# A third crossbar buffer, later chunk loads, and crossbar and store traffic counted in a static order: linear attention followed by a two-layer network

## The chip, the cores and the metric

The kernel runs on one core of a Trainium2 chip. The metric is the device time of one execution in microseconds (us), as the median of several runs. Five engines work side by side: TensorE (PE), VectorE (DVE), ScalarE (ACT), GpSimd (POOL) and SyncE (SP), which here only issues transfers. Each engine executes its own instruction list strictly in order, and so an instruction that waits holds up all that stands behind it on that engine.

## The reference, cut to what matters

```python
# q, k, v: (4, 8, 768, 64); blocks of 64 positions along the sequence
for b in range(nb):
    intra = einsum('bhic,bhjc->bhij', qb, kb) * Dmask      # lam ** (i - j), causal
    intra = einsum('bhij,bhjd->bhid', intra, vb)
    inter = einsum('bhid,bhde->bhie', qb * lam_pow, kv_state)
    out[:, :, sl] = intra + inter
    kv_state = lam_block * kv_state + einsum('bhsd,bhse->bhde', kb * rev_pow, vb)
x = out.transpose(0, 2, 1, 3).reshape(3072, 512)
h = x @ w_in                                                # 512 -> 2048
g = where(h >= 1, h, where(h <= -1, 0, (h + 1)**2 / 4))     # smoothed relu
result = g @ w_out                                          # 2048 -> 512, float32
```

## The kernel before, in words

The work is cut into 24 chunks of 128 positions (six for each of the four batches, all eight heads together) and six stages of 512 tokens (four chunks each). Attention produces a chunk's 128 columns of the transposed activations xT. The network then runs over the stages: L1 (f_l1, L368) multiplies by w_in into a PSUM tile ph, ACT applies the relu with bias (f_r, L376), DVE makes the smoothed relu of two such tiles in three instructions (f_g1 L382, f_g2 L386, f_g3 L401) into gT, and L2 (f_l2, L407) multiplies by w_out into py, which ACT copies out (f_y, L412) and SP stores (f_st, L416). An L1 item and an L2 item are each 2048 columns on PE; there are 96 of each.

The first four chunks are transposed on PE. Chunks 4 to 23 take another way, and these are what the change touches. SP loads k, q and v of the chunk (f_load, L450; names x1f, x0f, x2f; 256 KB each, six buffers of each). ACT (three quarters) and DVE (one quarter) cast k into a block-diagonal tile (f_ki, L262 and L264), DVE writes the scaled q beside it (f_qn, L267): together the tile kq, of which there are three. SP then issues one transpose through the DMA crossbar (f_xt, L273) from kq into a tile xq; the pool xtp has NXT = 2 of these. PE computes scores from xq (f_s, L324, eight matmuls of 64 columns), DVE masks them (f_m, L331, tile sc), and PE computes the chunk's output po from sc, v and the state (f_o, L349 and L351), reading xq once more. ACT copies po into xT (f_x, L358). Beside it, POOL scales v (cast_v, L281) and spreads it (f_vb, L284, tile vi), PE updates the state (f_u, L312) and ACT copies it out (f_ub, L315). So a tile of xq is free again when the output group of its chunk has run.

The order of every engine's instructions is fixed when the program is built. All operations are entered in a list by `add` with an engine, an estimated duration in ns, the operations they need, a due time, and `extra`, the latency after the engine is free again. run_plan then plays this list through: at each step it takes the engine that can start first, and on it the ready operation with the earliest due time. The order in which operations come out is the order of the program. Its clock exists only there; on the chip, engines wait on semaphores that come from the real dependencies. Besides the real engines there is an entry "DMA": operations with no instruction (`lambda: None`) that stand for the time that a transfer occupies the DMA engines, one after the other. In the kernel before only loads have such an entry. Due times come from l_due (one STEP = 1000 ns per L1 or L2 item, starting at T0), and o_due gives the due time of a chunk's output: LEAD before the L1 item that needs it. The line with `rel` (L224) holds operations back: a load may not be issued until 30000 ns before its chunk's o_due, a crossbar transpose not until 18000 before it.

The lines concerned, in short:

```python
add(("xt", c), "SP", 1800, ..., [("ki", c, ...), ("qn", c), ("s", c - NXT, 1), ("o", c - NXT)], due=-0.7, extra=4700)
add(("s", c, h), "PE", ..., [("kb", c), ("qT", c), ("xt", c), ...], due=od - 5500 + 2000 * h, extra=FILL)
add(("st", y), "SP", 650, ..., [("y", y), ("st", y - 1)], extra=1400, due=-1)
```

Of the kernel before, what the change touches and what calls it, by code (L numbers as in the profile page):

```python
# [23 lines left out]
def kernel(  # L24
# [37 lines left out]
    const = ctx.enter_context(tc.tile_pool(name="const", bufs=1))  # L62
    big = ctx.enter_context(tc.tile_pool(name="big", bufs=1))
    ld = ctx.enter_context(tc.tile_pool(name="ld", bufs=LD))
    NXT = 2
    qkp = ctx.enter_context(tc.tile_pool(name="qkp", bufs=3))
    ktp = ctx.enter_context(tc.tile_pool(name="ktp", bufs=2))
    xtp = ctx.enter_context(tc.tile_pool(name="xtp", bufs=NXT))
# [106 lines left out]
    def add(key, eng, ns, fn, needs=(), due=None, extra=0):  # L175
        OPS[key] = Op(key, eng, ns, fn, needs, due, extra)
        ops.append(OPS[key])

    def run_plan(free):

        users = {x.key: [] for x in ops}
        for x in ops:
            x.needs = [OPS[y] for y in x.keys if y in OPS]
            for y in x.needs:
                users[y.key].append(x)
        left = {x.key: len(x.needs) for x in ops}
        topo = [x for x in ops if not x.needs]
        for x in topo:
            for u in users[x.key]:
                left[u.key] -= 1  # L190
                if left[u.key] == 0:
                    topo.append(u)
        assert len(topo) == len(ops)
        for x in reversed(topo):
            d = [u.due - u.ns - x.extra - LAT for u in users[x.key] if u.eng not in ("DMA", "SP")]
            x.due = min(d + ([x.own] if x.own is not None else []), default=1e9)
            if x.eng in ("DMA", "SP") or x.key[0] in ("l1", "l2", "li", "wi", "zv"):
                x.due = x.own
        left = {x.key: len(x.needs) for x in ops}
        ready = {e: [] for e in free}  # L200
        for x in topo:
            if not x.needs:
                ready[x.eng].append((0, x))
        out_seq, pool_end = [], 0
        while len(out_seq) < len(ops):
            t, e = min((max(free[e], min(r for r, _ in lst)), e) for e, lst in ready.items() if lst)
            r, x = min(((r, x) for r, x in ready[e] if r <= t), key=lambda p: (p[1].due, p[0]))
            ready[e].remove((r, x))
            ns = x.ns
            if e == "DVE" and t < pool_end:  # L210
                if x.key[0] == "g1":
                    ns += pool_end - t
                elif x.key[0] in ("g2", "g"):
                    ns += min(ns, (pool_end - t) / 2)
            if e == "POOL":
                pool_end = t + ns
            free[e] = t + ns
            x.t, x.end = t, t + ns + x.extra
            out_seq.append((t, len(out_seq), x))
            for u in users[x.key]:  # L220
                left[u.key] -= 1
                if left[u.key] == 0:
                    lat = SLACK if u.eng == "PE" and x.end > 30000 else DSLACK if u.eng == "SP" else LAT
                    rel = o_due(u.key[1]) - 14000 if u.key[0] == "t" and u.key[1] >= CPS else o_due(u.key[1]) - 18000 if u.key[0] == "xt" and u.key[1] >= CPS else o_due(u.key[1]) - 30000 if u.key[0] == "li" and u.key[1] > SW else 0  # L224
                    ready[u.eng].append((max([rel] + [y.t if y.eng == u.eng else y.end + lat for y in u.needs]), u))
        pe_end = 1500
        for t, _, x in sorted(out_seq, key=lambda p: p[:2]):
            if x.eng == "PE":
                if x.key[0] == "l2":
                    pe_end = 1e9  # L230
                for _ in range(int((t - pe_end - 60) // (216 if t > 8000 else 430))):
                    nc.tensor.matmul(spin, lhsT=idle[:, 0:128], rhs=idle, start=True, stop=True)  # L232
                pe_end = max(pe_end, t + x.ns)
            if DBG:
                print(f"{t / 1e3:9.3f} {x.due / 1e3:9.3f} {x.eng:5s} {x.ns:6.0f} {x.key}")
            x.fn()
# [33 lines left out]
    def f_xt(c):  # L270
        t = xtp.tile([128, 3 * HP, 128], BF16, name="xq", tag="xq")
        kT[c], qT[c] = t[:, 0:2 * HP], t[:, 2 * HP:]
        nc.sync.dma_start_transpose(out=t, in_=kq[c % NKQ].rearrange("p a d -> p (a d)"))  # L273
# [136 lines left out]
    def f_y(s, ms):  # L410
        osb[s, ms] = op.tile([128, d_model], F32, name="osb", tag="osb")
        nc.scalar.copy(out=osb[s, ms], in_=py_t[s, ms])  # L412

    def f_st(s, ms):
        m0 = s * MS + ms * 128
        nc.sync.dma_start(out=out[m0:m0 + 128, :], in_=osb[s, ms])  # L416


    T0, STEP, LEAD = 24000, 1000, 3000
    PARTS = (4, 4, 4, 2, 2, 2)  # L420
    l1_order, l2_order = [], []
    for s in range(NST):
# [17 lines left out]
    def o_due(c):  # L440
        s, i = c // CPS, c % CPS
        w = CPS // PARTS[s]
        return l_due[1, s, 0, i // w] - LEAD - (w - 1 - i % w) * 8 * STEP
# [20 lines left out]
    for kind, i in order:  # L464
        for x in (1, 0, 2) if kind == "c" else (0,):
            sp = kind == "c" and not pool_ld(i, x)
            if kind == "w":
                key, land, ns, fn, need = ("wi", i), ("w", i), 2800, lambda i=i: load_w(i), []
            else:
                key, land, ns, fn = ("li", i, x), ("ld", i, x), 1060 if sp else 720 if i < 2 else 800, lambda i=i, x=x: f_load(i, x)  # L470
                need = [("cast", i - LD, x), *(("ki", i - LD, g, hi) for g in range(2) for hi in range(2) if x == 1), *(("cv", i - LD, g, hi) for g in range(2) for hi in range(2) if x == 2), ("qn", i - LD) if x == 0 else None, ("w", GATE[i]) if i in GATE else None]
            if not sp:
                need += fifo[-1:] + (landed[-RING:-RING + 1] if len(fifo) >= RING else [])
                fifo.append(key)
            elif i:
                need += splast
            if sp:
                splast = [key]
            add(key, "SP" if sp else "POOL", 600 if sp and i == 0 else 850 if sp else 900 if kind == "c" else 800, fn, need, due=0, extra=1250 if sp else 930)
            add(land, "DMA", ns, lambda: None, [key] + landed[-1:], extra=950 if sp and i == 0 else 1000 if kind == "c" and i < 2 else 3500 if kind == "c" and i < SW else 2000, due=0)  # L480
            landed.append(land)

# [7 lines left out]
    for c in range(NCH):  # L490
# [24 lines left out]
        if P:  # L515
            add(("t", c), "PE", mm(*[128] * 8), lambda c=c: f_t(c), [("cast", c, 0), ("cast", c, 1), ("kb", c - 1), ("qT", c - 1)], due=od - 9000, extra=FILL)
            add(("kb", c), "ACT" if c < KA else "DVE", 590 if c < KA else 430, lambda c=c: f_kb(c), [("t", c), ("s", c - 2, 1)])
            add(("qT", c), "DVE", 690, lambda c=c: f_qT(c), [("t", c), ("o", c - 3), ("qT", c - 1)] + [("tab", c // 2 * 2, hp) for hp in range(HP) if c < NCB])
        else:
            add(("xt", c), "SP", 1800, lambda c=c: f_xt(c), [("ki", c, 0, 0), ("ki", c, 0, 1), ("ki", c, 1, 0), ("ki", c, 1, 1), ("qn", c), ("s", c - NXT, 1), ("o", c - NXT)], due=-0.7, extra=4700)  # L520
        for j in range(1 if P else 0, 2):
            if (cb, j) == (NCB - 1, 1):
                continue
# [4 lines left out]
                add(("ub", c, j, hi), "ACT", 372, lambda c=c, j=j, hi=hi: f_ub(c, j, hi), [("u", c, j), ("o", (2 * c + j - NUB + 1) // 2)])  # L528
        for h in range(0 if P else 1, 2):
            add(("s", c, h), "PE", mm(*[128] * 4) if P else mm(*[64] * 8), lambda c=c, h=h: f_s(c, h),  # L530
                [("kb", c), ("qT", c), ("xt", c), ("m", c, 0) if h and P else ("m", c - 1, 1)],
                due=od - 5500 + 2000 * h, extra=FILL)
            add(("m", c, h), "DVE", 690, lambda c=c, h=h: f_m(c, h), [("s", c, h), ("o", c - 2), ("m", c, 0) if h else None])
        ub = [("ub", c - 1, 1, hi) for hi in range(2) if cb] + [("ub", c, 0, hi) for hi in range(0 if P else 2)]
# [18 lines left out]
    for n2, (s, ms, kg) in enumerate(l2_order):  # L553
        n = PARTS[s]
        need = [("g", n_of[s, 4 * kg + 4 - n, ms * n // CPS] // RW)]
        y = s * CPS + ms
        add(("l2", n2), "PE", mm(*[512] * 4), lambda a=(s, ms, kg): f_l2(*a),
            need + [("w", WS + kg), ("l2", n2 - 1), ("y", y - 2) if kg == 0 else None], due=l_due[2, s, ms, kg], extra=FILL)
        if kg == 3:
            add(("y", y), "ACT", 600, lambda a=(s, ms): f_y(*a), [("l2", n2), ("y", y - 1), ("st", y - 3)])  # L560
            add(("st", y), "SP", 650, lambda a=(s, ms): f_st(*a), [("y", y), ("st", y - 1)], extra=1400, due=-1)
    run_plan({"PE": 5500, "ACT": 4450, "DVE": 4650, "POOL": 2250, "DMA": 2700, "SP": 800})


# [28 lines left out]
```

## Time and profile before

| what | value |
|---|---|
| median of 5 runs | 227.93 us (224.24 to 230.06) |
| the profiled execution, its own time | 224.47 us |
| its span, first to last instruction | 222.3 us |
| mean granted TensorE clock | 0.996 |
| spin matmuls that fill PE's waits in the first 25 us (L232) | 38 instructions, 12.0 us |
| L1 matmuls (L368) | 97.5 us busy |
| L2 matmuls (L407) | 88.8 us busy |
| crossbar transposes (L273) | 20, 4.6 us median from issue to landing |
| loads of k, q, v by SP (L450) | 19 + 19 + 18, 3.8, 4.1 and 4.4 us to landing |
| stores (L416) | 24, 2.7 us to landing |

How to read it: the profile is one execution. An engine's busy time is the sum of its instructions. A row of waits reads "engine, tile, line <- what it waited for: us in total, times, longest". In the timeline a row is start, duration, engine, line, instruction, how many were merged, and in brackets the idle time ahead of it with what ended it. SPq is SP's queue: the duration of a row there is what SP needed to issue the transfer, not the transfer.

### The profile page before, as it was taken

What the parts mean: (1) busy time and instruction counts of PE and PEld (TensorE: products, weight loads), DVE (VectorE), ACT (ScalarE), POOL (GpSimd) and SP (SyncE); (2) the same over time, 40 slices, a digit from 0 to 9 for tenths busy, and PEclk for the clock granted to TensorE, in tenths of its full rate; (3) what the DMA queues carried; (4) which work ended last, traced back from release to release, by engine and by line L of the source; (5) the groups of instructions that cost most, each with busy time, mean ns of one, the idle gap of its engine ahead of it and who ended that gap; (6) DMA issues with size and microseconds to landing.
All of it is one profiled execution on the core that took longest, in us unless ns stands there. A gap on an engine that the chain in (4) does not pass through costs nothing.

```text
span 222.3 us, 5662 instructions
## 1 busy us (share of the span) xinstructions
PE 206.2 (93%) x2280; PEld 146.7 (66%) x2314; DVE 161.7 (73%) x237; ACT 150.0 (67%) x306; POOL 125.7 (57%) x160
## 2 busy tenths in 40 slices
PE   7789999899899996998799999998999999999993
PEld 2457888476477865886576766786676776666441
DVE  6535899966749986999998799899898546454200
ACT  6757576578588784987679877797678664555121
POOL 8989983369696997999655197467674000000000
PEclk9999999999999999999999999999999999999998
DMA  5999999999998999999568967669844520110112
GB/s 138 220 241 263 257 205 209 161 241 234 221 285 179 265 204 228 227 253 229 113 176 202 220 171 162 175 143 234 196 92 118 60 76 36 47 47 24 73 57 85
DMA packets 98729, 37.59 MB, mean 169 GB/s; under 512 B 90512, under 2 KB 94608, under 8 KB 98704
## 3 DMA queue, kind: packets, MB, share of 16 engines
q1 hardware_dynamic: 93056, 28.84, 58.0%
q0 software_dynamic: 5504, 8.39, 17.6%
q8 instruction: 18, 0.29, 0.5%
q14 instruction: 7, 0.06, 0.1%
q10 hardware_dynamic: 144, 0.00, 0.0%
HBM read 27.27 MB, written 6.29 MB: 151 GB/s over the span
## 4 chain that ended last, share of the span: by engine, by line
PE 62%; DVE 15%; DMA 13%; POOL 4%; issue 3%; ACT 1%; SPq 0%; POOLq 0%; ACTq 0%
PE py L407 28%; PE ph L368 26%; DMA w_out_sb<-in_moe_w_out_dram 5%; DMA w_in_sb<-in_moe_w_in_dram 4%; DVE gT L401 3%; DMA xq<-kq 3%; DVE w L386 3%; DVE t L382 3%; DVE sc L331 2%; DVE kq L267 2%; DVE kq L264 2%; PE po L351 2%; PE pu L312 2%; DMA x1f<-in_k_dram 1%; PE py L232 1%
## 5 line engine op out<-in xcount | busy, mean ns | idle before, releaser
L368 PE MATMUL ph<-xT,w_in_sb 128*128 128x128 bf16 (+1 forms) x1152 | 97.5, 237 | 0.5 <-DMA w_in_sb<-in_moe_w_in_dram 0.5
L407 PE MATMUL py<-w_out_sb,gT 128*128 128x512 bf16 x354 | 88.8, 379 | 1.7
L368 PEld LDWEIGHTS <-w_in_sb 128*128 128x128 bf16 x1152 | 80.9, 98 | 13.9 <-DMA w_in_sb<-in_moe_w_in_dram 0.7
L281 POOL TENSOR_TENSOR vn<-x2f,tab_k 64x256 bf16<-64x256 f32 x80 | 64.8, 810 | 39.4 <-DMA x2f<-in_v_dram 32.9
L376 ACT ACTIVATE r<-ph,one 128x512 bf16<-128x512 f32 x96 | 65.0, 687 | 30.4 <-PE ph L368 24.4
L407 PEld LDWEIGHTS <-gT 128*128 128x128 bf16 x384 | 35.0, 98 | 29.2 <-issue 0.2
L382 DVE TENSOR_SCALAR t<-r 128x1024 bf16<-128x1024 bf16 x48 | 27.3, 568 | 22.6 <-ACT r L376 22.4
L401 DVE TENSOR_TENSOR gT<-w,t 128x1024 bf16<-128x1024 bf16 x48 | 41.2, 858 | 1.5
L386 DVE TENSOR_TENSOR w<-r,t 128x1024 bf16<-128x1024 bf16 x48 | 38.7, 806 | 1.3
L284 POOL COPY vi<-vn 64x512 bf16<-64x512 bf16 x40 | 33.1, 827 | 2.2
L315 ACT CAST ubd<-pu 64x256 bf16<-64x256 f32 x80 | 29.1, 364 | 5.7 <-PE pu L312 2.7
L262 ACT CAST kq<-x1f 64x256 bf16<-64x256 f32 x60 | 24.1, 402 | 7.7 <-DMA x1f<-in_k_dram 3.8
L412 ACT COPY osb<-py 128x512 f32<-128x512 f32 x24 | 14.0, 584 | 13.1 <-PE py L407 11.9
L358 ACT CAST xT<-po 128x512 bf16<-128x512 f32 x24 | 14.1, 587 | 8.9 <-PE po L351 6.2
L267 DVE TENSOR_TENSOR kq<-x0f,tab_n 128x512 bf16<-128x512 f32 x20 | 18.6, 928 | 0.7 <-DMA x0f<-in_q_dram 0.4
L264 DVE TENSOR_TENSOR kq<-x1f 64x256 bf16<-64x256 f32 x20 | 12.2, 609 | 7.6 <-DMA x1f<-in_k_dram 4.8
L351 PE MATMUL po<-sc,vi 128*128 128x64 bf16 x160 | 11.8, 193 | 3.4 <-DVE sc L331 3.4
L331 DVE TENSOR_TENSOR sc<-ps,causal 128x512 bf16<-128x512 f32 x20 | 13.7, 685 | 1.4 <-PE ps L324 1.3
L232 PE MATMUL py<-idle 128*128 128x512 bf16 x38 | 12.0, 448 | 1.6 <-DVE one L119 1.2
L351 PEld LDWEIGHTS <-vi 128*128 128x128 bf16 x160 | 10.1, 98 | 4.2 <-DVE sc L331 1.8
L349 PEld LDWEIGHTS <-ubd 128*128 128x128 bf16 x148 | 10.0, 98 | 3.7 <-issue 1.9
L349 PE MATMUL po<-xq,ubd 128*128 128x64 bf16 x148 | 11.7, 193 | 0.0
(57 smaller groups left out, 109.7 us busy)
## 6 DMA issues: line engine op xcount, KB each, us to landing
out_dram<-osb SPq DMA_DIRECT2D x24, 256.0 KB, 2.7
x1f<-in_k_dram SPq DMA_DIRECT2D x19, 256.0 KB, 3.8
x0f<-in_q_dram SPq DMA_DIRECT2D x19, 256.0 KB, 4.1
x2f<-in_v_dram SPq DMA_DIRECT2D x18, 256.0 KB, 4.4
w_in_sb<-in_moe_w_in_dram POOLq DMA_DIRECT2D x4, 512.0 KB, 8.5
w_out_sb<-in_moe_w_out_dram POOLq DMA_DIRECT2D x4, 512.0 KB, 10.2
x2f<-in_v_dram POOLq DMA_DIRECT2D x6, 256.0 KB, 6.6
x1f<-in_k_dram POOLq DMA_DIRECT2D x5, 256.0 KB, 7.5
```

What stands on the lines that cost most here:

```text
L262: nc.scalar.copy(out=o, in_=i)
L267: nc.vector.tensor_tensor(kq[c % NKQ][:, 2 * HP:, :].rearrange("p a (b d) -> p (a b) d", b=2), qkv_ld[c, 0], _bc(tab_n[:, c % NCB, :], 2, ...
L281: nc.gpsimd.tensor_tensor(vn[c % NV][HD[hi], HP * g:HP * g + HP, :], quarter(qkv_ld[c, 2], g, hi), _bc(tab, 2, D), op=AX.mult)
L284: nc.gpsimd.tensor_copy(vi[c % NV][HD[hi], :, HD[hi]], vn[c % NV][HD[hi]])
L315: nc.scalar.copy(out=ubd[(2 * c + j) % NUB][HD[hi], :, HD[hi]], in_=pu[0][HD[hi], :, HD[hi] if c < NCB else HD[0]])
L351: nc.tensor.matmul(po[:, hp, HD[j]], lhsT=vi[c % NV][:, HP * j + hp, :], rhs=sc_sb[c, 1][:, hp, HD[j]], start=(cb == 0 and j == 0), stop=True)
L368: nc.tensor.matmul(ph[:, j * m:(j + 1) * m], lhsT=w_in_sb[:, ko, (i + j) * 128:(i + j + 1) * 128], rhs=xT[s][:, ko, p * m:(p + 1) * m], st ...
L376: nc.scalar.activation(out=r_t[grp][:, i, :], in_=ph_t[s, ni, part], func=AF.Relu, bias=one[:, 0:1])
L382: nc.vector.tensor_scalar(t_t[grp], r_t[grp], 0.5, 1.0, op0=AX.mult, op1=AX.min)
L386: nc.vector.tensor_tensor(w_t[grp], r_t[grp], t_t[grp], op=AX.subtract)
L401: nc.vector.tensor_tensor(o, w, t, op=AX.mult)
L407: nc.tensor.matmul(py_t[s, ms], lhsT=gT[s][:, ko, ms * 128:(ms + 1) * 128], rhs=w_out_sb[:, ko, :], start=(ko == 0), stop=(ko == FO - 1))
```

## The change

Nothing that is computed changes. The pool of crossbar outputs gets a third tile (NXT = 3). This also changes what the planner lets a transpose wait for: the scores and output of the chunk three before, in place of two before. LEAD grows from 3000 to 5000, so attention is due 2000 ns earlier against the L1 item that needs it. A transpose may be issued from 20000 ns before o_due (was 18000), a load from 26000 (was 30000). The SP cost of loads, transposes and stores in the plan falls (850 to 640, 1800 to 1450, 650 to 450). The transpose's flight, so far the `extra` of its SP entry (4700), becomes an entry of its own on "DMA" (2300, and 1800 until it lands), queued there with loads; scores need that entry. Stores get one as well (680), and a copy-out into an output buffer needs it.

```diff
-    NXT = 2
+    NXT = 3
...
-                    rel = o_due(u.key[1]) - 14000 if u.key[0] == "t" and u.key[1] >= CPS else o_due(u.key[1]) - 18000 if u.key[0] == "xt" and u.key[1] >= CPS else o_due(u.key[1]) - 30000 if u.key[0] == "li" and u.key[1] > SW else 0
+                    rel = o_due(u.key[1]) - 14000 if u.key[0] == "t" and u.key[1] >= CPS else o_due(u.key[1]) - 20000 if u.key[0] == "xt" and u.key[1] >= CPS else o_due(u.key[1]) - 26000 if u.key[0] == "li" and u.key[1] > SW else 0
...
-    T0, STEP, LEAD = 24000, 1000, 3000
+    T0, STEP, LEAD = 24000, 1000, 5000
...
-            add(key, "SP" if sp else "POOL", 600 if sp and i == 0 else 850 if sp else 900 if kind == "c" else 800, fn, need, due=0, extra=1250 if sp else 930)
+            add(key, "SP" if sp else "POOL", 600 if sp and i == 0 else 640 if sp else 900 if kind == "c" else 800, fn, need, due=0, extra=1250 if sp else 930)
...
-            add(("xt", c), "SP", 1800, lambda c=c: f_xt(c), [("ki", c, 0, 0), ("ki", c, 0, 1), ("ki", c, 1, 0), ("ki", c, 1, 1), ("qn", c), ("s", c - NXT, 1), ("o", c - NXT)], due=-0.7, extra=4700)
+            add(("xt", c), "SP", 1450, lambda c=c: f_xt(c), [("ki", c, 0, 0), ("ki", c, 0, 1), ("ki", c, 1, 0), ("ki", c, 1, 1), ("qn", c), ("s", c - NXT, 1), ("o", c - NXT)], due=-0.7, extra=1500)
+            add(("xd", c), "DMA", 2300, lambda: None, [("xt", c)], due=0, extra=1800)
...
-                [("kb", c), ("qT", c), ("xt", c), ("m", c, 0) if h and P else ("m", c - 1, 1)],
+                [("kb", c), ("qT", c), ("xd", c), ("m", c, 0) if h and P else ("m", c - 1, 1)],
...
-            add(("y", y), "ACT", 600, lambda a=(s, ms): f_y(*a), [("l2", n2), ("y", y - 1), ("st", y - 3)])
-            add(("st", y), "SP", 650, lambda a=(s, ms): f_st(*a), [("y", y), ("st", y - 1)], extra=1400, due=-1)
+            add(("y", y), "ACT", 600, lambda a=(s, ms): f_y(*a), [("l2", n2), ("y", y - 1), ("sd", y - 3)])
+            add(("st", y), "SP", 450, lambda a=(s, ms): f_st(*a), [("y", y), ("st", y - 1)], extra=1400, due=-1)
+            add(("sd", y), "DMA", 680, lambda: None, [("st", y)], due=0, extra=1000)
```

## The prediction, made before the changed kernel had run

> **What bounds the kernel now.** I read the page's busy times first, then the waits, then TensorE's timeline around each wait, then the SP queue's timeline and the queue's own waits, then busy times by stage. Engines first.
>
> ```profile
> PE 206.2 (93%) x2280; PEld 146.7 (66%) x2314; DVE 161.7 (73%) x237; ACT 150.0 (67%) x306; POOL 125.7 (57%) x160
> ...
> DMA  5999999999998999999568967669844520110112
> ```
>
> TensorE is the bound: 93% of the span, at full clock. Little is left to win, and it has to be won where PE idles. The DMA row says that the 16 DMA engines are full in slices 1 to 18, about 6 to 105 us, and half idle later. The list of waits shows what PE's idle time waits for (total us, times, longest):
>
> ```profile
> POOL vn L281 <- DMA x2f<-in_v_dram: 32.9, 12, 7.3
> ...
> PE ps L324 <- DMA xq<-kq: 3.8, 3, 2.1
> ...
> PE po L351 <- DVE sc L331: 3.4, 5, 1.3
> ```
>
> Beyond the prologue only two waits of PE matter: scores L324 on the crossbar output xq, 3.8 us, and outputs L351 on the masked scores sc from VectorE, 3.4 us. **7.2 us is the ceiling of what better order can give.** POOL's 32.9 us is four times larger and costs nothing by itself: its last product for a chunk is 8 to 22 us ahead of the PE group L351 that reads it. PE's timeline places the two biggest waits (start, us, instruction, idle before):
>
> ```profile
> 88.41 0.41 PE L324 MATMUL ps<-xq 128*128 128x64 bf16 x8 [2.14 <-DMA xq<-kq]
> ...
> 107.13 0.29 PE L351 MATMUL po<-sc,vi 128*128 128x64 bf16 x4 [1.31 <-DVE sc L331]
> ```
>
> The other two xq waits are 0.88 us at 42.54 (chunk 4) and 0.78 at 60.38 (chunk 6); 88.41 is chunk 10. Now the SP queue around them:
>
> ```profile
> 77.10 3.50 SPq L273 DMA_TRANSPOSE xq<-kq  x1
> 80.65 0.57 SPq L450 DMA_DIRECT2D x1f<-in_k_dram  x1
> 81.28 0.57 SPq L450 DMA_DIRECT2D x0f<-in_q_dram  x1
> 82.02 2.85 SPq L273 DMA_TRANSPOSE xq<-kq  x1
> ...
> 107.65 1.39 SPq L273 DMA_TRANSPOSE xq<-kq  x1
> 109.10 0.58 SPq L450 DMA_DIRECT2D x1f<-in_k_dram  x1
> ...
> 116.62 1.41 SPq L273 DMA_TRANSPOSE xq<-kq  x1
> ```
>
> Two regimes. From 36 to about 99 us SP has no gap: each entry starts about 0.1 us after the one before ended, an entry takes 0.4 to 3.6 us, and a transpose takes 4.6 to 6.3 us from issue to landing (10.9 for the first). Chunk 10's input kq was complete at 73.81 (end of L267), yet its transpose went out at 82.02 and landed 6.35 us later: it stood behind loads. From chunk 14 on SP has gaps, and a transpose goes out the moment the output group L351 of the chunk **two before** ends (107.65 is the end of chunk 12's, 116.62 of 13's, 128.9 of 15's, 133.6 of 16's): that is the reuse of two xq buffers. But there a transpose lands in 3.2 to 4.5 us and PE reads it 5.5 to 11 us after that, so this wait holds back SP, not PE. The stages:
>
> ```profile
> 60.00:89.00 29.00, 25.72 (x386) 20.21 (x392) 21.76 (x30) 21.01 (x46) 23.94 (x31) 1.00 1.04 236
> 89.00:122.00 33.00, 30.46 (x444) 24.04 (x449) 31.86 (x41) 27.61 (x59) 25.54 (x30) 1.00 0.84 199
> ```
>
> (columns PE, PEld, DVE, ACT, POOL, clock, DMA share, GB/s). In 89 to 122 us VectorE is busy 31.86 of 33.0 us: there it, not DMA, sets when sc is ready.
>
> **What the skill says.** The Trainium skill, "DMA: Bandwidth & Descriptors", Issuing engines are not separate DMA queues: all queues end on the same 16 engines and interleave. The trace agrees: L273 takes 4.6 to 6.3 us to land beside loads and 3.2 once the DMA row thins out. Same page, Why small descriptors are slow (HBM only): a fixed cost per packet makes 256-byte pieces costly; here 90512 of 98729 packets are under 512 B, and a 256 KB load takes 3.8 to 4.4 us. "Perfetto Trace Analysis", What "DMA-bound" means: a sequencer row that is solid DMA slices is itself a bound; that is SP from 36 to 99 us. "SBUF — State Buffer", Who interferes with whom: a VectorE instruction with two SBUF inputs contends with a GpSimd one that reads SBUF. L386 and L401 take 0.69 us or 0.98 us in the trace; it agrees in kind, and nothing in the change removes it.
>
> **The change part by part.** Instruction counts are equal (PE 4630 program rows in both, DVE 237, SP 102). The new "DMA" entries and changed costs issue nothing; they only move the order. The third buffer is 3 KB a partition (1536 bf16) and drops one wait. So all effect is order, read by laying the two programs' instruction orders beside each other. PE positions below are columns streamed before the instruction, in us at 0.417 ns a column (four 512-column L407 take 0.86 us in the trace); "loads" counts SP's L450 issues of chunks 6 and up ahead of the chunk's transpose.
>
> | chunk | loads before → after | PE position of L324, before → after |
> |---|---|---|
> | 4 | 0 → 0 | 33.07 → 33.92 |
> | 6 | 9 → 9 | 49.28 → 49.28 |
> | 7 | 14 → 12 | 57.07 → 53.44 |
> | 8 | 15 → 15 | 61.12 → 58.56 |
> | 9 | 21 → 18 | 69.87 → 66.45 |
> | 10 | 23 → 23 | 73.07 → 74.03 |
> | 11 | 27 → 24 | 82.56 → 80.00 |
> | 13 | 32 → 28 | 95.25 → 88.32 |
> | 15 | 36 → 33 | 107.09 → 100.27 |
> | 19 | 45 → 45 | 131.52 → 128.11 |
>
> Attention moves up to 6.9 us earlier in PE's order; transposes move past up to four loads, about 0.87 us each (71.03 to 77.10 holds six loads and one store: 6.07/7). DVE's casts L264/L267 stay within 1.5 us of their place, L331 moves with PE.
>
> *Chunk 4.* L324 goes behind one more L407 group (0.85): its wait of 0.88 falls to about 0.1. But L368 then follows L351 directly, while xT (L358) needs 0.59 us: a new wait of about 0.6. In return the w_out wait at 45.22 (0.24) goes. Sum about 0.
>
> *Chunks 6 to 9.* Transpose 6 goes out about 0.9 us earlier (one store fewer ahead, 0.53, and less load), and L331 of chunk 6 no longer stands behind a cast that waits for x1f until 61.83. Gain: 0.78 + 0.48 = 1.3. But 7 and 8 are now wanted 3.63 and 2.56 us of work sooner while their transposes come only about 3.4 and 0.9 us sooner: new waits of up to 1 and about 2 us. All of this is absorbed at chunk 10.
>
> *Chunk 10 decides the DMA-full stage.* Its transpose has the same 23 loads, 5 stores and 5 earlier crossbar entries after 36 us ahead of it. SP was gapless there, so I take the same landing, 88.4 us. PE then has 74.03 us of work behind it instead of 73.07: **gain 0.96 us**, wait 1.2 in place of 2.1 or, if PE comes later, less. Lower bound of this gain: -0.5 (crossbar traffic bunched); upper bound 2.1 plus the earlier 1.7, if transposes in fact run faster with fewer loads beside them (3.2 instead of 6 us to land).
>
> *Chunks 11 to 13.* From 88.4: transposes 11, 12, 13 would issue near 86, 91.6 and 95 us and land near 92, 97, 100.5; PE wants them at 80.00+14.4 = 94.4, 98.5 and 102.7. They fit with 1.5 to 2.4 us to spare. No gain from xq (there was no wait), none lost.
>
> *VectorE stage.* While PE waits for chunk 10, DVE before stood 2.01 us in L264, whose kq buffer the late transpose still read; after, that cast comes behind L331 and a whole group of three gate instructions (L382, L386, L401) comes first. At 88.4 DVE is then 1 to 1.7 us further on. sc waits behind that point were 0.86+1.31 and two smaller, about 2.9 of the 3.4. Taking DVE at its rate there (31.2 us of mean work done in 33.9), sc of chunk 11 ends near 96.3 as PE arrives, of chunk 12 about 1.2 us after PE arrives, the rest in time: **gain about 1.6 us**. Bounds: -1 (DVE work for sc simply pulled into the full stage) to 2.9.
>
> *Third buffer and later loads, chunk 14 on.* A transpose can go out 4 to 9 us sooner, but it had 5.5 us to spare: 0. What hides it is the PE work between landing and L324; PE's order takes 2 to 7 us of this cover away, so here the buffer only keeps the new order from waiting. Without it, chunk 15 (6.8 us earlier on PE, 6.4 to spare) would just wait. Loads come later in plan but SP stops standing at L273, so L281 waits do not grow; POOL has 8 us or more.
>
> *Tail.* From 168 us PE runs L368/L407 with no wait; unchanged.
>
> Sum: 0 + 0.96 + 1.6 = 2.6 us. Span 222.3 → 219.7; the profiled execution 224.47 → 221.9. The runs' median 227.93 is 3.5 above that execution; I scale it: 227.93 × 219.7/222.3 = **225.3 us**. About 2% is what a measurement of this kernel can tell from no change.
>
> **Rivals.**
> *Transposes really come free (0.26).* If order, not bytes, makes them slow, nearly all 7.2 us go and runs of 227.9 lose their extra waits too: 227.93 × 215.1/222.3 = 220.5. For it: landing 3.2 against 6 us. Against it: in 36 to 99 us the DMA engines are full whatever the order.
> *Hidden anyway (0.11).* The buffer wait is off the path, chunk 10 lands as before, DVE gives the microsecond back at chunk 12: 227.9. For it: spare of 5.5 to 11 us at chunks 14 on.
> *SP stands at a transpose whose input is late (0.13), the slower one.* After, from chunk 15, the loads of chunk c+2 are queued on SP behind transpose c, which waits for L262/L264/L267 of chunk c. Round trip: transpose issue 1.4, three loads 2.6, landing 4, casts with DVE's queue about 3: 11 us against 15.8 us of PE work for two chunks. Beyond 5 us of lateness each excess microsecond is paid once per two chunks, four times from 15 to 23; 1.5 excess cost 6 us: 233.9. It decides only if DVE falls 5 us further behind; nothing before shows that.
>
> **How the numbers follow.** Forecast 0.50 with its own range 223.4 to 228; rivals as given. Same is 0.50 + 0.11 = 0.61, faster 0.26, slower 0.13. The range 219.5 to 231.5 takes in the freed transposes down to its centre and the buffers' lower bounds, and leaves out most of the slow rival and the far end of the fast one.
>
> **What would show it.** Right: L324 still waits for xq near chunks 7 to 10, no xq wait later, sc waits about half, DVE still near full in 89 to 122 us, SP with gaps only after about 95. Transposes 14 on issued before the end of the output group two before. Wrong: no xq wait and landing under 5 us at 60 to 90 (rival one); x1f waits on DVE and ACT growing after 110 us (rival three); PE waits on xT or gT beyond chunk 4, which I hold for none.

## The result, and the profile after

The changed kernel takes **224.27 us** (median of 36 runs, 221.88 to 229.15) beside 225.96 us for the kernel before in the same sessions (71 runs): ratio 0.9964, 95% interval 0.9943 to 0.9984, so about 0.8 us less. The ratio leaves out disturbed runs, which is why it says less than the two medians (0.9925). The prediction was 225.3 us, from a median before of 227.93 us (five runs), so a ratio of 0.988. The profiled execution took 223.49 us and its span is 221.2 us, 1.1 us shorter than before.

The page of the changed kernel, in the same rows as before (busy us, then the tenths of the DMA engines' busy share in 40 slices):

```profile
PE 206.8 (93%) x2279; PEld 147.3 (67%) x2314; DVE 161.6 (73%) x237; ACT 150.1 (68%) x306; POOL 124.4 (56%) x160
...
DMA  5999999999999999999897888897964101110112
```

The work is the same on every engine. The DMA row has lost its hole: slices 19 to 26, counted from 0 (about 105 to 149 us), stood between 5 and 9 tenths before, and now at 7 to 9. Next the list of waits of the changed kernel:

```profile
POOL vn L281 <- DMA x2f<-in_v_dram: 31.0, 15, 7.5
...
DVE sc L331 <- PE ps L324: 7.8, 5, 2.9
...
PE ps L324 <- DMA xq<-kq: 2.6, 3, 1.8
...
DVE kq L264 <- DMA x1f<-in_k_dram: 2.1, 3, 0.9
...
PE po L351 <- DVE sc L331: 1.8, 4, 0.6
```

PE's wait for crossbar outputs fell from 3.8 to 2.6 us and that for masked scores from 3.4 to 1.8. That is 2.8 us less, yet the span fell by 1.1 only. Two waits of the list before are gone, those of the k casts for a kq tile that a late transpose still reads:

```profile
ACT kq L262 <- DMA xq<-kq: 3.2, 2, 2.7
...
DVE kq L264 <- DMA xq<-kq: 2.3, 2, 2.0
```

In their place VectorE stands 7.1 of its 7.8 us before 75 us, at the masks of chunks 6, 7 and 8, whose scores come late. PE's timeline (its rows with idle time ahead, 40 to 110 us) shows what took the rest:

```profile
45.48 1.95 PE L368 MATMUL ph<-xT,w_in_sb 128*128 128x128 bf16 x32 [0.68 <-ACT xT L358]
55.41 0.41 PE L324 MATMUL ps<-xq 128*128 128x64 bf16 x8 [0.56 <-DMA xq<-kq]
63.94 1.05 PE L368 MATMUL ph<-xT,w_in_sb 128*128 128x128 bf16 x16 [0.42 <-ACT r L376]
66.02 0.41 PE L324 MATMUL ps<-xq 128*128 128x64 bf16 x8 [0.17 <-DMA xq<-kq]
73.33 0.41 PE L324 MATMUL ps<-xq 128*128 128x64 bf16 x8 [1.83 <-DMA xq<-kq]
84.17 0.19 PE L351 MATMUL po<-sc,vi 128*128 128x64 bf16 x1 [0.42 <-DVE sc L331]
92.84 0.19 PE L351 MATMUL po<-sc,vi 128*128 128x64 bf16 x1 [0.55 <-DVE sc L331]
99.59 0.19 PE L351 MATMUL po<-sc,vi 128*128 128x64 bf16 x1 [0.47 <-DVE sc L331]
104.42 0.28 PE L351 MATMUL po<-sc,vi 128*128 128x64 bf16 x4 [0.34 <-DVE sc L331]
```

Two waits are new: 0.68 us on xT at chunk 4 and 0.42 on a relu. The longest xq wait sits at chunk 8 now (1.83), one stands at chunk 5 (0.56), and chunk 10's scores start at 89.99 with none. The part of the SP queue that decides this, of the changed kernel:

```profile
61.35 2.57 SPq L273 DMA_TRANSPOSE xq<-kq  x1
64.01 1.01 SPq L416 DMA_DIRECT2D out_dram<-osb  x2
65.12 0.41 SPq L450 DMA_DIRECT2D x1f<-in_k_dram  x1
65.62 0.65 SPq L450 DMA_DIRECT2D x0f<-in_q_dram  x1
66.37 1.28 SPq L450 DMA_DIRECT2D x2f<-in_v_dram  x1
67.82 3.51 SPq L273 DMA_TRANSPOSE xq<-kq  x1
...
83.33 2.56 SPq L273 DMA_TRANSPOSE xq<-kq  x1
...
102.13 1.78 SPq L273 DMA_TRANSPOSE xq<-kq  x1
...
108.86 1.39 SPq L273 DMA_TRANSPOSE xq<-kq  x1
...
116.74 1.39 SPq L273 DMA_TRANSPOSE xq<-kq  x1
```

67.82 is chunk 8's transpose. Its input was complete at 58.4 (end of its L267), so it stood 9.4 us behind chunk 7's transpose, stores and loads, and landed 5.5 us after its issue. 83.33 is chunk 10's, 1.31 us later than the 82.02 of before. The last three are those of chunks 14 to 16: the first two go out before the output group two chunks earlier has ended (104.93 and 109.35), so this reuse wait is gone. Chunk 16's waits for its own kq (L267 ends at 116.6). The two stages:

```profile
60.00:89.00 29.00, 25.83 (x378) 19.79 (x382) 20.60 (x27) 22.70 (x51) 21.38 (x30) 1.00 1.10 243
89.00:122.00 33.00, 31.26 (x482) 25.34 (x487) 31.21 (x43) 27.76 (x60) 24.79 (x30) 1.00 1.01 212
```

From 60 to 89 us PE is as busy as before (25.83 for 25.72): nothing was won where the DMA row is full. From 89 to 122 us it is busy 31.26 us for 30.46, with VectorE still at 31.21 of 33.

How far PE lags can be followed through the chunks: the start of L324 in the trace, less the PE work ahead of it in program order.

| scores of chunk | lag before, us | lag after | after less before |
|---|---|---|---|
| 4 | 9.47 | 9.09 | -0.38 |
| 6 | 11.10 | 11.40 | +0.30 |
| 8 | 12.41 | 14.77 | +2.36 |
| 10 | 15.34 | 15.96 | +0.62 |
| 13 | 18.75 | 18.44 | -0.31 |
| 23 | 21.72 | 20.68 | -1.04 |

Up to chunk 10 the changed kernel is 0.62 us behind. From there on it loses 4.72 us where the kernel before loses 6.38, and this 1.66 turns the loss into a gain of 1.04.

### The profile page after: what moved, and what is told of

The parts are those of the page before. It is cut to its first block, busy times and chain, and to the rows that moved or that the text cites. A ratio compares the mean times of both kernels' runs of the same rounds, so it can differ in the third digit from the quotient of the medians.

```text
span 221.2 us, 5669 instructions
## 1 busy us (share of the span) xinstructions
PE 206.8 (93%) x2279; PEld 147.3 (67%) x2314; DVE 161.6 (73%) x237; ACT 150.1 (68%) x306; POOL 124.4 (56%) x160
## 2 busy tenths in 40 slices
DMA packets 98729, 37.59 MB, mean 170 GB/s; under 512 B 90512, under 2 KB 94608, under 8 KB 98704
## 4 chain that ended last, share of the span: by engine, by line
PE 62%; DMA 17%; DVE 11%; issue 3%; POOL 3%; ACT 2%; SPq 0%; POOLq 0%; ACTq 0%
PE py L407 28%; PE ph L368 27%; DMA xq<-kq 10%; DMA w_in_sb<-in_moe_w_in_dram 4%; DVE w L386 3%; DMA x2f<-in_v_dram 2%; DVE t L382 2%; DVE gT L401 2%; DVE kq L267 2%; PE ps L324 2%; DMA out_dram<-osb 2%; DVE kq L264 2%; PE po L351 2%; PE pu L312 1%; PE po L349 1%
## 5 line engine op out<-in xcount | busy, mean ns | idle before, releaser
L368 PE MATMUL ph<-xT,w_in_sb 128*128 128x128 bf16 (+1 forms) x1152 | 97.1, 237 | 2.0 <-DMA w_in_sb<-in_moe_w_in_dram 0.9
L368 PEld LDWEIGHTS <-w_in_sb 128*128 128x128 bf16 x1152 | 80.6, 98 | 14.7 <-issue 1.5
L407 PE MATMUL py<-w_out_sb,gT 128*128 128x512 bf16 x353 | 87.7, 379 | 1.6
L281 POOL TENSOR_TENSOR vn<-x2f,tab_k 64x256 bf16<-64x256 f32 x80 | 63.0, 787 | 38.7 <-DMA x2f<-in_v_dram 31.0
L407 PEld LDWEIGHTS <-gT 128*128 128x128 bf16 x384 | 35.4, 98 | 30.4
L401 DVE TENSOR_TENSOR gT<-w,t 128x1024 bf16<-128x1024 bf16 x48 | 40.3, 840 | 1.5
L386 DVE TENSOR_TENSOR w<-r,t 128x1024 bf16<-128x1024 bf16 x48 | 40.2, 837 | 1.4
L315 ACT CAST ubd<-pu 64x256 bf16<-64x256 f32 x80 | 29.1, 364 | 8.7 <-PE pu L312 5.7
L267 DVE TENSOR_TENSOR kq<-x0f,tab_n 128x512 bf16<-128x512 f32 x20 | 16.9, 846 | 0.7 <-DMA x0f<-in_q_dram 0.5
L264 DVE TENSOR_TENSOR kq<-x1f 64x256 bf16<-64x256 f32 x20 | 13.3, 663 | 2.6 <-DMA x1f<-in_k_dram 2.1
L351 PE MATMUL po<-sc,vi 128*128 128x64 bf16 x160 | 11.7, 193 | 1.8 <-DVE sc L331 1.8
L351 PEld LDWEIGHTS <-vi 128*128 128x128 bf16 x160 | 10.2, 98 | 1.6 <-issue 0.5
```

The source lines that it names most:

```text
L281: nc.gpsimd.tensor_tensor(vn[c % NV][HD[hi], HP * g:HP * g + HP, :], quarter(qkv_ld[c, 2], g, hi), _bc(tab, 2, D), op=AX.mult)
L315: nc.scalar.copy(out=ubd[(2 * c + j) % NUB][HD[hi], :, HD[hi]], in_=pu[0][HD[hi], :, HD[hi] if c < NCB else HD[0]])
L351: nc.tensor.matmul(po[:, hp, HD[j]], lhsT=vi[c % NV][:, HP * j + hp, :], rhs=sc_sb[c, 1][:, hp, HD[j]], start=(cb == 0 and j == 0), stop=True)
L368: nc.tensor.matmul(ph[:, j * m:(j + 1) * m], lhsT=w_in_sb[:, ko, (i + j) * 128:(i + j + 1) * 128], rhs=xT[s][:, ko, p * m:(p + 1) * m], st ...
L386: nc.vector.tensor_tensor(w_t[grp], r_t[grp], t_t[grp], op=AX.subtract)
L401: nc.vector.tensor_tensor(o, w, t, op=AX.mult)
```

## The experiments

In the expectations T is the reading of the prediction (the new order pays through chunk 10's transpose and through VectorE, the third buffer as such does nothing), and the R are rivals to it. T2 and R4 are about the accounting, T3 and R5 about the slow first transpose, R6 about ScalarE. All ratios are to the kernel before, run in the same session, with 95% intervals; the changed kernel was timed in other sessions than the runs below it, so that two rows are compared only through the kernel before. The last column is the time of the one execution that was profiled (the kernel before: 224.47); it need not be typical of its row.

| run | ratio | interval | profiled, us |
|---|---|---|---|
| the change (after) | 0.9964 | 0.9943 to 0.9984 | 223.49 |
| third buffer only | 1.0137 | 1.0074 to 1.0199 | 229.73 |
| order of after, two buffers | 0.9928 | 0.9868 to 0.9988 | 222.48 |
| accounting only | 1.0138 | 1.0087 to 1.0189 | 228.20 |
| after, loads even later | 0.9994 | 0.9938 to 1.0050 | 228.51 |
| after, long rows | none, too few runs | | 222.10 |
| before, long rows | 0.9846 | 0.9722 to 0.9970 | 224.81 |
| after, less VectorE work | 0.9880 | 0.9849 to 0.9911 | 225.26 |
| before, less VectorE work | 0.9890 | 0.9845 to 0.9935 | 224.15 |
| all but the accounting | 0.9882 | 0.9848 to 0.9916 | 223.46 |
| after, last weight load early | 0.9976 | 0.9915 to 1.0037 | 224.86 |
| after, k cast all on ScalarE | 0.9994 | 0.9950 to 1.0038 | 225.32 |
| later loads only | 0.9924 | 0.9892 to 0.9956 | 224.88 |

### Is it the third buffer?

The kernel before with one number changed:

```diff
-    NXT = 2
+    NXT = 3
```

> The kernel before with a third crossbar buffer (pool and plan), nothing else. Theory (T): the buffer wait held back SP, not TensorE; alone the buffer only lets the plan pull attention further ahead (chunk 10's scores at PE position 67.1 us of work instead of 73.1, with 20 loads and 4 stores ahead of its transpose instead of 23 and 5). Four entries fewer are worth about 3.5 us of SP, the scores come 6 us sooner, so the wait at chunk 10 grows by about 2.5 us and later sc waits give back about 1: 0.5 to 2.5 us slower than before. Rival R1 (the third buffer is where the gain comes from): at least 0.8 us faster than before.

And the changed kernel, its program order kept, with two tiles in the pool:

```diff
-    xtp = ctx.enter_context(tc.tile_pool(name="xtp", bufs=NXT))
+    xtp = ctx.enter_context(tc.tile_pool(name="xtp", bufs=2))
```

> The changed kernel with its instruction order kept, and a pool of two crossbar tiles. T: transposes of chunks 11 to 14 and a few later ones go out up to 4 us later, but TensorE reads them with 5 us to spare: within 0.5 us of the changed kernel, so still 0.3 to 1 us faster than before. My prediction's side remark (chunk 15 would wait for its transpose) would cost up to 0.4 us. R1: gives the whole gain back, so equal to before or slower.

The buffer alone is about 3.1 us slower than before, a little beyond T's 0.5 to 2.5. The planner, told of three buffers, puts chunk 10's scores at 67.09 us of PE work in place of 73.07, with 20 loads ahead of their transpose. T's longer wait at chunk 10 is not in the profile, though: of 8.0 us of waits for xq, 6.51 are at chunk 4, where the order is still that of before and the first transpose took 16.4 us to land; chunks 8 and 10 wait 0.75 and 0.76 us. PE lags 5.57 us more than before at chunk 4 and 5.33 at chunk 23. So where the 3.1 us arise stays open. The order of after with two tiles is as fast as with three, the intervals overlap, and its longest waits are of the same kind and size as those of after:

```profile
PE po L351 <- DVE sc L331: 3.0, 6, 1.0
...
PE ps L324 <- DMA xq<-kq: 2.3, 1, 2.3
```

So the third tile as storage neither costs nor gives anything that these runs can tell (the interval is 0.6% to either side). R1, that it carries the gain, falls, if by a narrow margin: the interval ends at 0.9988. The profile agrees, with no wait for xq behind chunk 8, and from chunk 4 to chunk 23 PE loses 11.46 us with two tiles and 11.59 with three. The same number in the plan, alone, comes with a loss; in two orders that also hold loads back (after, and all but the accounting) there is none.

### Is it the accounting?

The kernel before with the new entries and costs, but NXT 2, LEAD 3000 and the old release times:

```diff
-... ("xt", c), "SP", 1800, ... extra=4700)
+... ("xt", c), "SP", 1450, ... extra=1500)
+            add(("xd", c), "DMA", 2300, lambda: None, [("xt", c)], due=0, extra=1800)
...
+            add(("sd", y), "DMA", 680, lambda: None, [("st", y)], due=0, extra=1000)
```

> The kernel before with only the plan's accounting changed (crossbar and store traffic on the DMA row, lower SP costs); two buffers, LEAD 3000, old release times. The plan then puts chunk 10's scores at PE position 75.6 instead of 73.1 with 24 loads ahead of its transpose instead of 23. T: the transpose lands 0.9 us later and is wanted 2.6 us later, so the xq wait at chunk 10 falls from about 2 to 0.5 us; outputs now sit close before the L368 that needs them (0.2 us of other work at chunk 13), so 0.5 us of waits on xT come back: 0.5 to 1.5 us faster than before. R1: no change, as the buffers are still two.

A miss: about 3.1 us slower where T had said faster. By the program's order 12 loads stand ahead of chunk 6's transpose (9 before), 24 ahead of chunk 9's (21) and 29 ahead of chunk 11's (27). ACT's timeline in this run shows the costliest consequence,

```profile
85.80 1.24 ACT L262 CAST kq<-x1f 64x256 bf16<-64x256 f32 x3 [4.44 <-DMA xq<-kq]
86.94 0.74 ACT L315 CAST ubd<-pu 64x256 bf16<-64x256 f32 x2
```

and PE's timeline what it leads to:

```profile
87.74 0.29 PE L312 MATMUL pu<-vn,kq 128*128 128x64 bf16 x4 [3.35 <-ACT ubd L315]
```

Chunk 12's cast has to write a kq tile that chunk 9's late transpose still reads. ACT stands 4.44 us in that cast; the state copies L315 are queued behind it, and PE stands 3.35 us for them. A late transpose can thus be paid for twice: by the scores that read it, and by whatever is queued behind the next writer of its input. I had looked at DVE's queue for this and not at ACT's.

Then the reverse, all of the change but the accounting:

```diff
-    NXT = 2
+    NXT = 3
...
-    ... o_due(u.key[1]) - 18000 ... o_due(u.key[1]) - 30000 ...
+    ... o_due(u.key[1]) - 20000 ... o_due(u.key[1]) - 26000 ...
...
-    T0, STEP, LEAD = 24000, 1000, 3000
+    T0, STEP, LEAD = 24000, 1000, 5000
```

> The kernel before with the third buffer, LEAD 5000 and the new release times, but the old accounting (no crossbar or store entries on the DMA row, old SP costs). Chunk 10's scores come at PE position 70.6 with 21 loads and 5 stores ahead of its transpose; chunk 9's at 62.0 with 15 loads. Theory (T2: what counts is how much SP has ahead of a transpose against where PE wants its scores): two loads fewer, about 1.7 us, against scores 2.5 us sooner than before: the wait for xq in chunks 7 to 10 is about 1 us longer than before, and sc waits about 1 shorter as in the changed kernel: 0 to 1.5 us slower than the kernel before, so accounting is worth 1 to 2 us beside the rest although alone it costs 3. Rival R4 (accounting is harmful, the rest carries the gain): at least 1 us faster than before.

0.9882, about 2.7 us under the kernel before (median 223.4 us of 22 runs beside 225.49). Its interval lies below that of after, so **it beats the kernel before and probably the changed one too**: by the medians of all runs the two are closer, at 0.9907 and 0.9925 of before. T2 had it 0 to 1.5 us slower than before and misses; R4 holds. Its waits and its SP queue:

```profile
PE ps L324 <- DMA xq<-kq: 2.3, 3, 1.3
...
PE po L351 <- DVE sc L331: 1.4, 2, 1.1
```

```profile
60.59 2.35 SPq L273 DMA_TRANSPOSE xq<-kq  x1
65.76 2.65 SPq L273 DMA_TRANSPOSE xq<-kq  x1
```

Chunk 8's transpose goes out at 65.76 instead of 67.82, with 13 loads ahead of it and not 15, and PE waits 0.42 us for it where after waits 1.83. Two L407 groups stay between L351 and L368 at chunk 4, so PE's wait for xT is gone as well. Its profiled span, 221.6, is no shorter than after's. It started late: PE waited 1.50 us for w_in at 20.45, where after waited 0.76, and came to chunk 4's scores with 1.47 us more lag than after. From there to chunk 23 it loses 10.15 us, after 11.59 and before 12.24; but a late start by itself takes some later waits away, so the 22 runs carry the verdict, not this one execution.

### Is it the later loads?

Release times alone, in the kernel before:

```diff
-    ... o_due(u.key[1]) - 18000 ... o_due(u.key[1]) - 30000 ...
+    ... o_due(u.key[1]) - 20000 ... o_due(u.key[1]) - 26000 ...
```

> The kernel before with only the two release times changed: loads from 26000 (was 30000) and transposes from 20000 (was 18000) ns before the output's due time; two buffers, LEAD 3000, old accounting. Ahead of the transposes of chunks 7, 9, 10 and 11 stand 12, 18, 21 and 24 loads instead of 14, 21, 23 and 27, while PE wants their scores within 1.7 us of where it did. Theory T2 (the place of a transpose in SP's queue against PE's order): the xq waits of chunks 6 to 10 shrink from 2.9 to under 1.5 us; sc waits stay about 3: 1 to 2.5 us faster than the kernel before, so as good as the changed kernel or better. Rival (late loads only pay together with LEAD and the third buffer): within 0.7 us of the kernel before.

And loads held back further, in the changed kernel:

```diff
-    ... o_due(u.key[1]) - 26000 ...
+    ... o_due(u.key[1]) - 24000 ...
```

> The changed kernel with loads released 24000 instead of 26000 ns ahead of the output's due time. Chunk 10's scores keep PE position 74.0, but 21 instead of 23 loads stand ahead of its transpose. T (chunk 10 waits for what SP has to issue ahead of it): its transpose goes out 1.7 us earlier, the wait of about 1.8 us at chunk 10 falls under 0.4, and the kernel is 0.8 to 1.8 us faster than the changed one. Rival R2 (the DMA engines' total work, not the place in the queue, sets the landing): the landing moves by less than 0.5 us and so does the time.

The one line is worth about 1.7 us (0.9924), as T2 had it: ahead of transposes 7, 9, 10 and 11 stand 12, 18, 21 and 24 loads, where before there are 14, 21, 23 and 27. It is the loads that do it: with the transposes' release left at 18000 the planner puts out the same order. With its earlier attention and third buffer on top (all but the accounting) it is 0.9882; the two intervals overlap, so LEAD's own share is not settled. Held back further, nothing more is won: T's 0.8 to 1.8 us did not come. PE's timeline of this second run, after the first transpose, has no xq wait at all, but waits for VectorE:

```profile
85.67 0.19 PE L351 MATMUL po<-sc,vi 128*128 128x64 bf16 x1 [0.74 <-DVE sc L331]
96.01 0.19 PE L351 MATMUL po<-sc,vi 128*128 128x64 bf16 x1 [1.28 <-DVE sc L331]
```

Its list of waits has 4.6 us for sc (six times) where after has 1.8, and that of the run with later loads only has 5.0:

```profile
PE po L351 <- DVE sc L331: 5.0, 5, 1.9
```

This reads as if VectorE took back what transposes stop costing, but it is argued, not shown. In the second run the first transpose took 15.0 us, and PE, 3.7 us later at chunk 4 than in after, had less to wait for. In the first, the profiled execution is no faster than that of before, so it does not show where the 1.7 us come from.

### Is it VectorE?

DVE's quarter of the k cast does one pair of heads in place of four, in both kernels, so part of k is left out of the result:

```diff
-            nc.vector.tensor_tensor(o, i, i, op=AX.max)
+            nc.vector.tensor_tensor(o[:, 0:1], i[:, 0:1], i[:, 0:1], op=AX.max)
```

> The changed kernel with VectorE's quarter of the k cast writing one head pair of four (part of the k tile stays stale, output not the reference's); order unchanged. It takes about 0.4 us off VectorE for each of 20 chunks. T: in 89 to 122 us VectorE sets when sc is ready, so sc waits of TensorE fall from 1.8 us to under 0.8, and the kernel is 0.5 to 1.5 us faster than the changed one; the xq wait at chunk 10 stays. Rival: sc waits come from scores being late, not from VectorE: no change.

> The kernel before with the same smaller cast (output not the reference's). T: sc waits fall from 3.4 us to under 1.5, 1 to 2.5 us faster than before, more than the changed kernel gains from it: part of the change's gain is relief of the same queue. Rival: no more than the changed kernel gains.

Before becomes 2.5 us faster, after 1.9 more; the two do not differ beyond their intervals, so that the change relieves the same queue is not shown. Less VectorE work is worth as much as the best reordering, in either order: in time it is a bound in its own right, as T says. The way T gave is not shown. The cast fell only from 0.61 to 0.44 us in before and from 0.66 to 0.45 in after, not by 0.4. The sc waits went from 3.4 to 2.2 us in before (T: under 1.5) and from 1.8 to 1.6 in after (T: under 0.8), and both profiled executions took longer than the median of their runs (224.15 beside 222.98, 225.26 beside 222.58). A cast that ends sooner also completes kq and frees VectorE for the gate sooner; what each is worth was not separated. Nor can the work just be handed on. The changed kernel with the k cast all on ACT:

```diff
-    KE = ('ACT', 'ACT', 'ACT', 'DVE')
+    KE = ('ACT', 'ACT', 'ACT', 'ACT')
```

> The changed kernel with all four quarters of the k cast on ScalarE (a full kernel; the plan is made anew). VectorE is relieved of 0.61 to 0.66 us for each of 20 chunks, ScalarE gets 0.40. T (VectorE sets sc from 89 us on): like the run with the smaller cast, 1 to 2 us faster than the changed kernel, sc waits under 1 us; chunk 10 still waits for xq. Rival R6: ScalarE, at 67 to 68 percent, delays relu and state copies, and the new order puts 27 loads ahead of chunk 11's transpose: no faster than the changed kernel.

0.9994, no faster than before and no gain on after, as R6 had it. The sc waits fall to 0.4 us, and PE waits for ACT's relu instead (the order is another one here, so not all of this need be the moved casts):

```profile
PE ph L368 <- ACT r L376: 3.7, 2, 2.9
```

### Does the order matter only while DMA is full?

The same bytes loaded as 128 rows of 2048 B in place of 256 B pieces, in both kernels; heads land in the wrong places, the number of bytes is the same, and the packets fall from 98729 to 48553:

```diff
-        d = e.dma_start(out=t, in_=src.rearrange("h p d -> p h d"))
+        src = bass.AP((q, k, v)[x].tensor, c * C * H * D, [[H * D, C], [1, H * D]])
+        d = e.dma_start(out=t.rearrange("p h d -> p (h d)"), in_=src)
```

> The changed kernel, same order and bytes, but every load of q, k, v takes 128 contiguous rows of 2048 bytes instead of eight times 256 bytes a row; the data are other positions of the same tensors, so the output is not the reference's. T (the crossbar waits of chunks 4 to 10 come from DMA engines and SP filled by small packets): loads land in about 2.5 instead of 4 us, SP has gaps before 99 us, xq waits of TensorE go from 2.6 us to under 0.5; span 1.5 to 3 us shorter than the changed kernel. Rival R2b (transposes are slow by themselves, or PE's order is the bound): xq waits stay above 2 us.

> The kernel before with the same long rows (output not the reference's). T: xq waits vanish here too, and what remains between this and the long-row changed kernel is the VectorE part: sc waits of about 2 to 3 us here against 1 to 2 there, so this one 0.5 to 1.5 us slower than the long-row changed kernel. Rival R3 (the order only matters when DMA is full): the two are equal within 0.5 us.

Before: 0.9846, in four runs. After: a median of 223.22 us in four runs, the lowest 220.11, too few for a ratio, and so no more than "about equal". In both profiles PE's only wait for xq is that of chunk 4 (5.74 us before, 1.49 after); in that of after the median landing of a transpose falls from 4.7 to 3.7 us, SP has gaps from 63 us, and sc waits grow to 3.6. (In that of before, PE came to chunk 4 4.2 us later than without long rows, and this alone may hide later waits.) The loads themselves hardly land sooner: 3.5, 4.0 and 3.9 us in place of 3.7, 4.0 and 4.4, where T expected 2.5. What gets shorter is SP's part: from 45 to 100 us the median issue of a load takes 0.42 us in after in place of 0.67, and SP is idle for 18.6 us in place of 0.7. So the queue that the order was to shorten is gone, and R3, that the order matters only then, fits as far as so few runs tell. R2b falls, and so does the 0.5 to 1.5 us by which before was to stay behind: it has fewer sc waits (2.1 us) than after. Whether fewer packets help through SP's issues or through the DMA engines was not separated.

### Why is the first transpose so slow?

It took 11.0 us to land in after, the later ones 3.2 to 6.1. The changed kernel with the eighth w_out load issued right behind the seventh:

> The changed kernel with the eighth weight load (512 KB of w_out) issued by GpSimd right behind the seventh, near 27 us instead of 34.6; all other orders unchanged. In ten profiles so far the first crossbar transpose (issued at 31 to 32 us, just ahead of that load) took 9.8 to 16.4 us to land, against 3.2 to 6.3 for all later ones. T3 (it shares the DMA engines with that weight load and a v load): it lands in under 9 us, TensorE's wait at chunk 4 vanishes, the runs spread less and the median falls 1 to 2 us against the changed kernel. Rival R5 (the first transpose is slow for a reason of its own): it still takes 10 us and more; no change in time.

0.9976, and 15.6 us to land. T3, that this load holds it up, falls. The traces say more than the expectation did. Its "3.2 to 6.3 for all later ones" does not hold: other runs had 7.1, and with long rows the second transpose, issued at 43.3 and 43.4 us, took 10.9 and 8.9. Nor is it only the transpose: in after, all that is issued from 31 to 41 us takes 9 to 11 us to land, the loads of k, q and v by SP (9.4, 9.9 and 9.2) and the v load by GpSimd (9.1) too. With the weight load early, that load and the k and q loads behind it take 16 us, where they took 10.8 to 11.6. So it is a crowded stretch, not a slow transpose; which transfers fill it stays open.

## Why the prediction was right, point by point

- **The time.** 225.3 predicted, 224.27 measured. That they are so close is luck in part: the forecast stood on five runs of the kernel before with a median of 227.93 us, and 71 runs have 225.96. As a gain, 1.2% was forecast and 0.4% measured; in the profiled execution, 2.6 us of span and 1.1. The side was right, and of the two places of the gain the second; the size was not. Nor is 2% what these runs can tell from no change: most intervals are 0.2 to 0.6% to either side.
- **VectorE stage, +1.6.** Measured 1.66 behind chunk 10. The sc waits there fell from 2.96 to 1.36 us, and VectorE's 2.01 us at L264 are gone: in after it has no idle row from 78 to 111 us. The runs with less VectorE work show that this engine's work costs time; that it does so through these waits they don't show.
- **Chunk 10, +0.96: the mis-sized term.** Measured -0.62, just outside its bounds (lower bound -0.5). The prediction took the landing as 88.4 because the same entries stood ahead of it. They did, but from chunk 4's transpose to chunk 10's they took 51.4 us (31.96 to 83.33) in place of 50.4, and it landed at 89.4: equal contents of the queue did not make equal times. This did not decide, however. PE came only at 89.99, without waiting, because of what it had lost at chunks 5 to 8, so an earlier landing would have given nothing.
- **Chunks 6 to 9, "absorbed at chunk 10".** The new wait at chunk 8 was about as forecast (2 predicted, 1.83 idle; chunk 7: up to 1 predicted, 0.17). But it wasn't absorbed. PE lags 2.36 us more at chunk 8 and still 0.62 more at chunk 10, whose transpose no longer held it up: a loss can be absorbed only as far as a later wait reaches, and by the prediction's own sum only 1.2 us of wait were left there. Transposes 7 and 8 did not come 3.4 and 0.9 us sooner, but 2.0 sooner and 0.4 later. And SP's entries take 0.4 to 3.6 us, as the prediction read them, with one exception: the v load at 38.23 took 6.16.
- **Chunk 4, 0.** The xT wait came (0.6 predicted, 0.68 idle), the xq wait fell to 0.11. Chunk 5's wait of 0.56 was missed: seven loads stand ahead of its transpose where six did, and my table had left that row out.
- **Chunks 11 to 13.** No xq wait, as forecast; the transposes went out at 87.27, 92.37 and 96.36 (86, 91.6 and 95 forecast).
- **Third buffer, 0.** Shown, within 0.6%: the same order with two tiles is no slower. My remark that chunk 15 would then wait isn't borne out. The sign "transposes 14 on before the end of the output group two before" holds for 14, 15, 22 and 23 only; from 16 to 21 a transpose waits for its own kq and goes out after that end. That the buffer as a number in the plan comes with a loss of 3 us by itself was not in the prediction.
- **The rivals.** Transposes did not come free (landing 5.5 to 6.1 us at chunks 8 and 10). SP does stand at transposes with late input, 24.0 us in ten waits for L267 from 95 us on (3.6 before), but not long enough to matter: DVE waits for x1f 2.1 us in all, ACT 1.1, all of it before 89 us. "Hidden anyway" is nearer than its 0.11 says, with 0.8 of 226 us.
- **Not in the prediction at all:** that the accounting, which issues nothing, costs. With it the change is at 0.9964, without it at 0.9882. What the profiles show of it is chunk 8's transpose 2 us later and the missing cover at chunk 4, which the accounting alone brings too (0.68 us for xT); how the 1.8 us split between these, chunk 5 and the rest stays open.

## What to carry to other kernels

When one in-order queue without gaps issues both loads and transfers that an engine waits for, count the loads ahead of each such transfer, chunk by chunk and without skipping rows: issuing loads later was worth more than the buffer and the finer accounting. A cost model that describes the hardware more fully can still give a worse order, so undo each part of a planner change alone and keep the best subset. A loss at one wait is made good only by a longer wait behind it, so follow the lag of the busiest engine through the stages before adding up gains. And look at where in time a profile differs before explaining a run by its order: the profiled execution with only the third buffer had lost its time where its order was still the old one.

## What the runs showed of the hardware that was not expected

The first crossbar transpose, issued at 31 to 33 us, needed 9.2 to 16.4 us to land in fourteen profiles of near-identical programs, while all later ones but the two named above need 3.2 to 7.1; the loads issued beside it are as slow. In those with 14 us or more PE stood 3.3 to 6.5 us at chunk 4, so this crowded stretch probably carries part of the spread between runs of one kernel (argued from profiles, not tested). From 36 to 40 us the kernel before moved only 116 GB/s, at a DMA share of 1.67 by the trace, and from 40 to 44 us 190 GB/s at 0.95: busy is not the same as moving data. A row length of 2048 B in place of 256 B took a transpose's median landing from 4.7 to 3.7 us in after and from 4.6 to 3.4 in before, although the transposes themselves were not touched. And the gate's two-input instructions have two lengths: L386 takes 0.98 us (median of 24 in before) where a GpSimd instruction runs beside it for over 30% of its time, and 0.69 (22) where none does.
